# Half a crossed product on ScalarE and GpSimd, and an earlier issue of weights, in a convolution with a recurrent transformer behind it

## The chip, the cores and the metric

The kernel runs on one core of one Trainium2 chip. The metric is the device time of one execution in microseconds.

## The reference, cut to what matters

Two independent heads; their outputs are joined along the last axis. Head A is a transformer with a recurrent memory: 64 segments of 32 rows, one behind the other, each with 8 rows of memory that the segment before has left. Head B is a long convolution of `u` with a kernel that comes from a state-space model, done over the frequency domain, plus a skip.

```
# A: for s in range(64):
h = concat([mem, xs]);  q, k, v = h @ Wq, h @ Wk, h @ Wv      # 1024 -> 32 heads x 128
o = softmax(mask(q @ k.T * scale)) @ v;  o = o @ Wo           # 4096 -> 1024
mem = o[:, :8];  outs.append(o[:, 8:])
# B: L = 2048, D = 1024, N = 128
K = einsum(Cc, exp(dt * A * l), dt * Bc).real                 # [D, L]
y = irfft(rfft(pad(u.T)) * rfft(pad(K)))[:, :L].T + u * Dskip
```

## The kernel before, in words

The program is written out by hand: each engine does its instructions in the order in which the Python code issues them, and semaphores are added wherever an instruction reads or overwrites what an earlier one, in that order, has written or still reads. Head B comes first (`part_b`), with the projections of A's rows that need no memory woven in; head A follows (`part_a`, from about 577 us on).

In `part_b` the spectrum of `u` is made by matmuls and kept in DRAM (`Ud`); that of the convolution's kernel is made block by block: 16 blocks of 256 columns and a quarter of the frequencies (`b`, `dq`, `kc`). Each block has two pairs of frequency classes, `n_` = 0 and 1. The loop over `b` (L1542) does the following.

- `spectrum(b + 1, n_, ...)` (L1221) on TensorE: 20 matmuls into a PSUM tile `pa` of 128 x 1024 float32 (two banks, `ps_e` with two tiles and `ps_h` with one). The left operand is a forward matrix `G[kc]`, three fifths of which are scaled first on VectorE by `weighted` (L1206); that is done once for each `kc`, in blocks 0 to 3.
- `pointwise(b, now)` (L1461) is a generator in two stages. The first stage multiplies the block's spectra by that of `u`: `times_u` (L1384) makes for each pair the crossed product `Zs[:, n_]` (the imaginary part of `u` times the tile) and then, in place, the straight one. `rotate` (L1389) joins both into a complex product, for pair 0 into `even` (named `y` in the profile). `load_u` (L1214) then fetches `u` for the next block into `uq[0]` and `uq[1]` (`wq` in the profile). The second stage, behind a `yield`, rotates pair 1 in place, forms a difference (`od`) and a sum (`y`) on VectorE, and has GpSimd spread them into bfloat16 tiles `Bt` by four operations (L1486 to L1489).
- From block 4 on `inverses(b - 4, n_)` on TensorE goes back to time: 16 or more matmuls, the skip through an identity, and an eviction on ScalarE (L1538). ScalarE's queue also issues the store of the rows.
- `skips` on GpSimd multiplies rows of `u` by `Dskip`.

Where the second stage is run depends on the block. For `b < 3` it comes ahead of the second spectrum of `b + 1`; for `b >= 3` it comes behind both spectra.

SyncE's queue (SP) carries nearly all loads, in order: `u`'s spectrum, `u`'s rows for the skips (`load_pair`, L1496), the inverse matrices `MI`, and the weights of head A. These are 512 KB tiles that stay in SBUF for all segments; `residents` (L1679) is a generator that issues one at each `next(resident)`, into memory that head B has done with. Behind it come four streamed buffers `wst` (L1704 to L1706), then eight tiles in the place of `MI`.

In `part_a` a segment goes through `quads` for q, k and v and `oproj` for the output; `unit` (L300) gives the weight tile for a key, from SBUF or, for twelve keys, streamed from DRAM by `stage` (L337). In the first segment it also loads the resident tiles that had no room before. Three tiles are kept in PSUM as bits (`load_kept`, L343): for the key `("q", 0, 7)` the right half is kept so, through a `wst` buffer, and the left half lies in `a_half`. Both are loaded in the first segment, where the key `("q", 0, 2)` is asked for.

Of the kernel before, what the change touches and what calls it, by code (L numbers as in the profile page):

```python
# [10 lines left out]
BF16 = mybir.dt.bfloat16  # L11
F32 = mybir.dt.float32
I32 = mybir.dt.int32
I16 = mybir.dt.int16
ALU = mybir.AluOpType
# [249 lines left out]
def load_resident(tc, pool, src, key, W_res, eng=None, t_=None):  # L265
    if t_ is None:
        t_ = pool.tile([128, 2048], BF16, name="W_%s" % "_".join(str(i) for i in key))
    (eng or tc.nc.sync).dma_start(out=t_[:].rearrange("e (h d) -> e h d", h=2) if key[0] == "o" else t_[:], in_=src(key))
    W_res[key] = t_


def part_a(ctx, tc, x, src, WD, HE, seg_len, out_a, ahead, W_res, rest, places, first):
# [17 lines left out]
    ctx.enter_context(tc.manual_schedule())  # L290
    ctx_w = rest.ctx
    wst = ahead.wst
    wres = ctx_w.enter_context(tc.tile_pool(name="a_wres", bufs=1, side="right"))

    loads = [SLOTS]
# [4 lines left out]
    def unit(key):  # L300
        if key in rest:

            rest.remove(key)
            load_resident(tc, wres, src, key, W_res, None, places.pop(0)() if places else None)
        if key in W_res:
            return W_res[key]
        if key in KEPT:
            return ahead_of.pop(key) + halves.get(key, [])
        between.pop(key, lambda: None)()
        if key in first:  # L310
            return first.pop(key)
        if key[0] == "v":
            for k_ in rest[0:3 if key[1] == 0 else 1]:
                rest.remove(k_)
                load_resident(tc, wres, src, k_, W_res)
        return stage(key, WD[key][:])

    ctx_l = ctx_w.enter_context(ExitStack())
# [24 lines left out]
    def load_kept(key):  # L343
        kept[key] = {}
        for n in (1,) if key in HALF else (0, 1):
            kept[key][n] = ps_k.tile([128, 512], F32, name="keep", tag="keep%d" % sum(len(b) for b in kept.values()))
        if key in HALF:
            w = wst.tile([128, 2048], BF16, name="wst", tag="w%d" % (loads[0] % SLOTS))
            loads[0] += 1
            h_ = ahead.low["half"] if key[0] == "q" else wres.tile([128, 1024], BF16, name="Whalf")  # L350
            for n, t_ in ((1, w[:, 0:1024]), (0, h_[:])):
                nc.sync.dma_start(out=t_, in_=src(key)[:, n, :] if key[0] == "o" else src(key)[:, 1024 * n:1024 * n + 1024])
            words(kept[key][1][:], w[:, 0:1024])
            halves[key] = [(0, 1024, h_)]
        else:
            t_ = first.pop(key)
            for n in (0, 1):
                words(kept[key][n][:], t_[:, 1024 * n:1024 * n + 1024])
# [47 lines left out]
    for s in range(NS):  # L406
# [123 lines left out]
        a = quads("k", 0, (0, 2, 4, 6, 1, 3, 5, 7))  # L530
# [3 lines left out]
        a = quads("q", 0, range(0, 6))  # L534
# [178 lines left out]
def part_b(ctx, tc, u, A_re, A_im, B_re, B_im, C_re, C_im, log_dt, Dskip, out_b, ahead, copies, residents, first_state):  # L713
# [667 lines left out]
        t_ = pool.tile([128, 2, 512], F32, name="pa", tag="pa")  # L1381
        return [t_[:].rearrange("p h (c d) -> p h c d", c=2)]

    def times_u(s_, Z, n_, X=None):  # L1384
        us = uq[n_].rearrange("p (a c d) -> p a c d", a=2, c=2)
        for i, t_ in ((1, Z), (0, s_[n_][0] if X is None else X)):
            v.tensor_tensor(out=t_, in0=us[:, :, i, :].unsqueeze(2).to_broadcast([128, 2, 2, DQ]), in1=s_[n_][0], op=ALU.mult)  # L1387

    def rotate(Y, X, Z):  # L1389
        v.tensor_tensor(out=Y[:, :, 0, :], in0=X[:, :, 0, :], in1=Z[:, :, 1, :], op=ALU.subtract)  # L1390
# [45 lines left out]
    iv = ctx.enter_context(tc.tile_pool(name="b_iv", bufs=2))  # L1436
    bp = ctx.enter_context(tc.tile_pool(name="b_B", bufs=1))
    ctx2 = ctx.enter_context(ExitStack())
    pw = ctx2.enter_context(tc.tile_pool(name="b_pw", bufs=1))
    bp0 = ctx2.enter_context(tc.tile_pool(name="b_B0", bufs=1))  # L1440
    out_v = out_b.rearrange("(c p r) d -> r p c d", p=128, r=4)
    u_v = u.rearrange("(c p r) d -> r p c d", p=128, r=4)
# [3 lines left out]
    places = [wsl[3][:], wsl[0][:], g0[:, 6144:8192], XT[:, 2048:4096], XT[:, 0:2048]] + [g0[:, 2048 * i:2048 * i + 2048] for i in range(3)]  # L1446
    resident = residents(pool, places + [XT[:, 2048 * i:2048 * i + 2048] for i in range(2, 10)], [t_[:] for t_ in wsl[1:3]], [k1[:, 2048 * i:2048 * i + 2048] for i in range(2)])

    Zs, even = (pw.tile([128, *dims], F32, name=nm) for nm, dims in (("z", (2, 2, 2, DQ)), ("y", (2, 2, DQ))))

    def blocks(t_):
        return t_.rearrange("p i c d -> p (i c) d")
# [8 lines left out]
    def pointwise(b, s_):  # L1461
        dq, kc = b // 4, b % 4
        if b:
            times_u(s_, Zs[:, 0], 0)
            if b < 4:
                rotate(even, s_[0][0], Zs[:, 0])
                if b < 3:
                    weighted(b + 1, 0, amps[b + 1])
                load_u(b + 1, (0,))
                for i in {1: (0,), 2: (4,), 3: ()}[b]:  # L1470
                    load_inverse(i)
                if b == 1:
                    next(resident)
            times_u(s_, Zs[:, 1], 1)
            if b < 15:
                load_u(b + 1, (1,) if b < 4 else (0, 1))
            if b > 3:
                rotate(even, s_[0][0], Zs[:, 0])
        yield
        if b:  # L1480
            rotate(s_[1][0], s_[1][0], Zs[:, 1])
        Y = (even[:], s_[1][0]) if b else (first[:, 0], first[:, 1])
        v.tensor_tensor(out=odd[:], in0=Y[0], in1=Y[1], op=ALU.subtract)
        v.tensor_tensor(out=even[:], in0=Y[0], in1=Y[1], op=ALU.add)
        for i, op in ((0, ALU.add), (1, ALU.subtract)):
            gp.tensor_tensor(out=spectra(dq, kc, 0)[:, i], in0=even[:, 0], in1=even[:, 1], op=op)  # L1486
        eng, to = v if b == 15 else gp, blocks(spectra(dq, kc, 1))
        eng.tensor_tensor(out=to[:, 0:4:3], in0=odd[:, 0], in1=odd[:, 1, ::-1], op=ALU.add)
        eng.tensor_tensor(out=to[:, 2:0:-1], in0=odd[:, 0], in1=odd[:, 1, ::-1], op=ALU.subtract)  # L1489
# [52 lines left out]
    for b in range(16):  # L1542
        points = pointwise(b, now)
        next(points)
        for _ in range(4 if b in (2, 3) else 0):
            second.pop(0)()
        if b == 2:
            ks.append([])
        if 2 <= b < 6:
            lo, hi = b - 2, min(b - 1, 3) if b < 5 else 5  # L1550
            ks[1].extend(load_k(1, k1[:, DH * lo:DH * hi], lo))
        if b >= 4:
            load_pair(b - 2, iv)
        if b == 3:
            v.tensor_scalar(out=ident[:], in0=ident[:], scalar1=float(PLEN / 2), scalar2=None, op0=ALU.mult)
            load_pair(0, iv)
            load_pair(1, iv)
            state = first_state(g0[0:8, 5120:6144], iv.tile([128, 8, 24], BF16, name="xt0", bufs=1))
            next(state)
            ctx_k.close()  # L1560
            ps_h = ctx.enter_context(tc.tile_pool(name="b_psh", bufs=1, space=PSUM))
            ps_y = ctx.enter_context(tc.tile_pool(name="b_psy", bufs=2, space=PSUM))
        if b == 0:
            now = nxt_
        elif b + 1 < 16:
            now = []
            for n_ in range(2):
                if b < 3 and n_:
                    next(points, None)
                    weighted(b + 1, 1, amps[b + 1])  # L1570
                now.append(halves(ps_h if b > 2 and (2 * b + n_) % 3 == 0 else ps_e))
                spectrum(b + 1, n_, [now[n_][0][:, half] for half in range(2)], (3,) * 7 if b == 1 else ())
                if b >= 4:
                    inverses(b - 4, n_)
        next(points, None)
        for n_ in (0, 1) if b == 3 else (b - 2,) if 3 < b < 15 else ():
            skips(n_, gp)
        for i in {1: (1,), 3: (5,), 4: (2, 3), 5: (6, 7)}.get(b, ()):
            load_inverse(i)
        if b == 2:  # L1580
            rows4 = g0[0:4, 5120:6144]
            for half in range(2):
                sy.dma_start(out=rows4[:, DH * half:DH * half + DH], in_=Kx[half][31, NF - 1].rearrange("g c -> (g c)").partition_broadcast(4))
            sy.dma_start(out=w4, in_=u[0:4, :])
            gp.tensor_tensor(out=w4, in0=rows4[:, 0:D], in1=w4, op=ALU.mult)
            gp.memset(l4, 0.0)
            gp.memset(l4[:, :, 127:128], float(PLEN / 2))
            gp.affine_select(out=l4[:, :, 127:128], in_=l4[:, :, 127:128], compare_op=ALU.is_ge, fill=0.0, base=0, pattern=[[1, 4], [0, 1]],
                             channel_multiplier=-1)
        for _ in range({1: 2, 2: 2, 3: 1, 4: 1, 5: 1, 6: 2, 7: 2, 8: 2, 9: 2, 11: 3, 12: 3, 13: 2, 14: 3, 15: 3}.get(b, 0)):  # L1590
            next(resident)
        if b == 10:
            state.send(ps_y.tile([128, 8, 128], BF16, name="yp", tag="yp")[:, :, 0:8])
# [3 lines left out]
    for n_ in range(3):  # L1597
        inverse_begin(3, PAIRS[n_], begun[n_ // 2][:, n_ % 2])
    ctx2.close()
    last = ctx.enter_context(tc.tile_pool(name="b_last", bufs=1))  # L1600
    load_pair(14, iv)
    load_pair(15, last, 1)
    for _ in range(4):
        next(resident)
    for n_ in range(8):
        if n_ > 0 and n_ % 2 == 0:
            skips(12 + n_ // 2, v)
        inverses(12 + n_ // 2, n_ % 2)
        if n_ == 1:
            next(state)  # L1610
        next(resident)
# [32 lines left out]
def kernel(  # L1644
# [34 lines left out]
    def residents(stay, early, uqs, last):  # L1679
# [8 lines left out]
        for t_ in some(stay, "KT1", 2):  # L1688
            put(t_)
            yield  # L1690
        for t_ in early:
            put(t_)
            yield
        put(last[0])
# [79 lines left out]
```

## Time and profile before

| | |
|---|---|
| three runs | 1917.59, 1918.08, 1934.71 us; median 1918.08 |
| the profiled execution | 1915.11 us; span of its instructions 1913.4 us |
| busy, share of the span | PE 92%, DVE 71%, PEld 57%, ACT 48%, POOL 27% |
| mean granted TensorE clock | 0.986 |
| DMA | 594.21 MB, mean 311 GB/s |
| frequency loop, blocks 0 to 15 | about 405 to 560 us |
| head A's 64 segments | from about 577 us to the end |

In a row of the timeline stand the start in us from the span's start, the duration in us, the engine, the line of the kernel, the operation, what it writes and reads, shapes, how many instructions were merged, and in brackets how long the engine had been idle and what ended that. PE is TensorE, PEld its weight load, DVE VectorE, ACT ScalarE, POOL GpSimd, SP SyncE; a q behind the name is the engine's queue that issues a DMA. In a row of one line's instructions stand the shortest, median and longest duration in ns. In a row of the windows stand for each engine the busy us and the number of instructions, then the granted share of TensorE's clock, the share of the 16 DMA engines that were busy and what they moved in GB/s.

### The profile page before, as it was taken

The numbers are of one execution on the slowest core, as the hardware profiler recorded it, in microseconds if no ns is written. First come the engines' busy times: TensorE is split into PE (matmuls) and PEld (weight loads), VectorE is DVE, ScalarE is ACT, GpSimd is POOL, SyncE is SP. The second block draws the span as 40 slices with busy tenths as digits, with TensorE's granted clock in tenths as the row PEclk, the third lists the DMA queues.
The fourth block names the chain that finished last, engine by engine and source line by source line (L and its number), as shares of the span: only waits on it lengthen the run. The fifth ranks groups of instructions, "written<-read, shape, count | busy, mean of one in ns | idle before, by whom it ended". The sixth has DMA issues, their size and how long they took to land.

```text
span 1913.4 us, 73735 instructions
## 1 busy us (share of the span) xinstructions
PE 1768.3 (92%) x31563; PEld 1088.4 (57%) x31563; DVE 1349.7 (71%) x3367; ACT 921.2 (48%) x1655; POOL 514.4 (27%) x900
## 2 busy tenths in 40 slices
PE   8999999868986989999999999999999999999989
PEld 3666665546773555555555555555555555555554
DVE  8599999899973666666666666766666666666650
ACT  8799999860112434444343444444343444444420
POOL 2354544427770111111111111111111111212120
PEclk9999999898998999999999999999999999999999
DMA  7889898778799999999999999999999999999993
GB/s 220 238 236 266 258 276 249 219 220 293 258 306 357 348 322 342 341 345 337 344 353 344 338 350 351 336 355 343 340 348 354 330 345 346 346 340 347 352 335 95
DMA packets 341744, 594.21 MB, mean 311 GB/s; under 512 B 94100, under 2 KB 216476, under 8 KB 339368
## 3 DMA queue, kind: packets, MB, share of 16 engines
q1 hardware_dynamic: 297944, 534.99, 81.8%
q10 hardware_dynamic: 36816, 29.59, 4.8%
q0 software_dynamic: 6656, 24.92, 3.5%
q8 instruction: 247, 4.05, 0.8%
q14 instruction: 81, 0.66, 0.1%
HBM read 531.92 MB, written 71.63 MB: 315 GB/s over the span
## 4 chain that ended last, share of the span: by engine, by line
PE 46%; DMA 31%; DVE 12%; ACT 5%; issue 3%; POOL 2%; SPq 1%; DVEq 0%; POOLq 0%; ACTq 0%
PE acc L414 22%; DMA wst<-WD_v 11%; DMA wst<-WD_o 9%; PE pp L527 9%; DMA wst<-WD_q 3%; PE pe L667 3%; DMA wst<-WD_k 2%; PE tr L425 2%; PE pro L184 2%; DVE nr L1274 1%; PE pro L197 1%; DMA arena<-PKd 1%; PE pv L495 1%; DMA wq<-Ud 1%; DVE pa L1387 1%
## 5 line engine op out<-in xcount | busy, mean ns | idle before, releaser
L414 PEld LDWEIGHTS <-a_hT 128*32 128x32 bf16 x12351 | 329.6, 96 | 327.3 <-issue 76.1
L420 ACT CAST arena<-acc 128x512 bf16<-128x512 f32 x384 | 225.2, 586 | 395.1 <-PE acc L414 326.8
L414 PE MATMUL acc<-wst,a_hT 128*32 128x512 bf16 x2308 | 230.1, 382 | 35.3 <-DMA wst<-WD_v 26.1
L527 PEld LDWEIGHTS <-arena 128*32 128x32 bf16 x8256 | 215.4, 96 | 76.9 <-issue 53.6
L428 POOL COPY arena<-arena 128x128 bf16<-128x128 bf16 x128 | 37.6, 294 | 697.6 <-PE tr L425 364.9
L335 DVE TENSOR_SCALAR arena<-keep 128x256 int32<-128x256 int32 x508 | 174.3, 395 | 27.9 <-PE acc L414 27.9
L414 PE MATMUL acc<-XM,a_hT 128*32 128x512 bf16 x2560 | 184.2, 380 | 0.0
L414 PE MATMUL acc<-W,a_hT 128*32 128x512 bf16 x1536 | 132.8, 384 | 0.0
L197 PE MATMUL pro<-XM,wsl 128*128 128x512 bf16 x512 | 124.6, 387 | 2.6 <-DVE kst L206 1.5
L454 DVE TENSOR_REDUCE a_mx<-sc 128x4 f32<-128x160 f32 (+1 forms) x192 | 71.8, 374 | 74.2 <-PE sc L442 72.9
L527 PE MATMUL pp<-W_o,arena 128*32 128x256 bf16 x3584 | 121.7, 273 | 2.3 <-issue 2.2
L544 DVE COPY arena<-tr 128x512 bf16<-128x512 bf16 x64 | 27.2, 425 | 126.3 <-PE tr L425 126.3
L458 ACT ACTIVATE sc<-sc 128x160 f32<-128x160 f32 (+1 forms) x192 | 63.9, 333 | 106.5 <-DVE sc L455 106.0
L462 DVE TENSOR_REDUCE a_mx<-sc 128x4 f32<-128x160 f32 (+1 forms) x192 | 72.7, 379 | 55.2 <-ACT sc L458 54.9
L489 POOL TENSOR_TENSOR arena<-arena,a_BD 128x128 bf16<-128x128 bf16 x128 | 51.3, 401 | 211.5 <-DVE arena L472 201.3
L414 PE MATMUL acc<-W_q,a_hT 128*32 128x512 bf16 x1536 | 107.9, 379 | 0.0
L1274 DVE TENSOR_SCALAR nr<-ptt 128x456 f32<-128x456 int16 x128 | 80.3, 628 | 31.3 <-PE ptt L1252 28.3
L1266 ACT ACTIVATE E<-pa 128x648 bf16<-128x648 f32 x128 | 87.7, 712 | 16.9 <-PE pa L1258 15.2
L623 ACT CAST arena<-pp 128x128 bf16<-128x128 f32 x64 | 17.0, 266 | 154.8 <-DVE arena L623 154.8
L527 PE MATMUL pp<-wst,arena 128*32 128x256 bf16 x1536 | 76.4, 274 | 16.4 <-DMA wst<-WD_o 15.0
L513 ACT CAST arena<-pv 128x512 bf16<-128x512 f32 (+1 forms) x128 | 61.4, 479 | 59.6 <-PE pv L499 33.4
L425 PEld LDWEIGHTS <-arena 128*128 128x128 bf16 x1024 | 57.6, 98 | 54.8 <-issue 25.9
(334 smaller groups left out, 3967.7 us busy)
## 6 DMA issues: line engine op xcount, KB each, us to landing
wst<-WD_v SPq DMA_DIRECT2D x256, 512.0 KB
wst<-WD_k SPq DMA_DIRECT2D x192, 512.0 KB
wst<-WD_o SPq DMA_DIRECT2D x192, 512.0 KB
wst<-WD_q SPq DMA_DIRECT2D x128, 512.0 KB
Ud<-ux POOLq DMA_DIRECT2D x16, 1024.0 KB, 7.5
wq<-Ud SPq DMA_DIRECT2D x32, 512.0 KB
wsl<-in_A_Wk_dram SPq DMA_DIRECT2D x16, 512.0 KB
wsl<-in_A_Wv_dram SPq DMA_DIRECT2D x16, 512.0 KB
```

Of the source, the lines that this page charges most:

```text
L197: nc.tensor.matmul(a[:], lhsT=w[:, kc, 128 * j:128 * j + 128], rhs=xTl[:, kc, :, :].rearrange("p s k -> p (s k)"), start=(kc == 0), stop=( ...
L335: nc.vector.tensor_scalar(out=out.bitcast(I32), in0=in_.bitcast(I32), scalar1=0, scalar2=None, op0=ALU.bitwise_or)
L414: nc.tensor.matmul(a[32 * g:32 * g + 32, o_:o_ + rhs.shape[1]], lhsT=hT[:, kc, :], rhs=rhs, start=(kc == 0), stop=(kc == KC - 1), tile_pos ...
L420: nc.scalar.copy(out=q, in_=a[:])
L425: nc.tensor.transpose(out=p[:, hl, :, :].rearrange("p a b -> p (a b)"), in_=q[:, 128 * hl:128 * hl + 128], identity=ident[:])
L454: nc.vector.tensor_reduce(out=m_, in_=x, axis=AX.X, op=ALU.max)
L458: nc.scalar.activation(out=flat(sc, i), in_=flat(sc, i), func=ACT.Exp, scale=scale)
L462: nc.vector.tensor_reduce(out=m_, in_=x, axis=AX.X, op=ALU.add)
L513: copy(out=o[:, i:i + n], in_=p[:, i:i + n, :].rearrange("p a (g q) -> p a g q", g=4))
L527: nc.tensor.matmul(po[32 * qt:32 * qt + 32, o_:o_ + rhs.shape[1]], lhsT=oT[:, h % 4, (h % 16) // 4, :], rhs=rhs, start=False, stop=(h == 3 ...
L1266: sc.activation(out=T["E", r, e // 4][:, lo:lo + 8 * NE].rearrange("p (i c) -> p i c", i=2), in_=T.pop(("p", r, e))[:, :, 0:4 * NE], func= ...
L1274: v.tensor_scalar(out=T["n", r, e // 4][:, lo:lo + 8 * NT], in0=T.pop(("t", r, e))[:, 0:8 * NT].bitcast(I16)[:, 0:16 * NT:2], scalar1=floa ...
```

## The change

1. `times_u` makes for pair 1 only the first half of the crossed product on VectorE (`parts=1`). The other half, `Zs[:, 1, 1]`, is made by two new functions: `moved` has ScalarE copy that half of the spectrum from PSUM, and `shared` has GpSimd multiply it in place by `u`. For block 1 both are issued in the turn `b == 0`; for later blocks `moved` is issued behind the second spectrum of `b + 1`, and `shared` ahead of the second stage of block `b` from `b = 3` on, behind it for `b` = 1 and 2.
2. `weighted(b + 1, 0, ...)` in blocks 1 and 2 moves behind the products of both pairs; from block 4 on `load_u` of the first half is issued directly behind the products of pair 0.
3. `Zs` and `even` get pools of their own, `even` first. The four streamed buffers are issued ahead of the last two `load_pair`; the last of these uses the ring of four instead of a pool of its own.
4. The left half of `("q", 0, 7)` is loaded by `residents` in `part_b`, ahead of the sixth tile of `early`. The first five resident tiles that `part_a` loads beside streamed v tiles go to a new pool `a_wout`.

```diff
+    wout = ctx_w.enter_context(tc.tile_pool(name="a_wout", bufs=1, side="right"))
+    outs = [wout.tile([128, 2048], BF16, name="W_o", tag="W%d" % i) for i in range(5)]
...
-                load_resident(tc, wres, src, k_, W_res)
+                load_resident(tc, wres, src, k_, W_res, None, outs.pop(0) if outs else None)
...
-            for n, t_ in ((1, w[:, 0:1024]), (0, h_[:])):
+            for n, t_ in ((1, w[:, 0:1024]), (0, h_[:]))[0:1 if key[0] == "q" else 2]:
...
-    def times_u(s_, Z, n_, X=None):
+    def times_u(s_, Z, n_, X=None, parts=2):
         us = uq[n_].rearrange("p (a c d) -> p a c d", a=2, c=2)
-        for i, t_ in ((1, Z), (0, s_[n_][0] if X is None else X)):
-            v.tensor_tensor(out=t_, in0=us[:, :, i, :].unsqueeze(2).to_broadcast([128, 2, 2, DQ]), in1=s_[n_][0], op=ALU.mult)
+        for i, m, t_ in ((1, parts, Z), (0, 2, s_[n_][0] if X is None else X)):
+            v.tensor_tensor(out=t_[:, 0:m], in0=us[:, 0:m, i, :].unsqueeze(2).to_broadcast([128, m, 2, DQ]), in1=s_[n_][0][:, 0:m], op=ALU.mult)
+
+    def moved(s_):
+        sc.copy(out=Zs[:, 1, 1], in_=s_[1][0][:, 1])
+
+    def shared():
+        us = uq[1].rearrange("p (a c d) -> p a c d", a=2, c=2)
+        gp.tensor_tensor(out=Zs[:, 1, 1], in0=us[:, 1, 1, :].unsqueeze(1).to_broadcast([128, 2, DQ]), in1=Zs[:, 1, 1], op=ALU.mult)
...
-    pw = ctx2.enter_context(tc.tile_pool(name="b_pw", bufs=1))
+    py, pw = (ctx2.enter_context(tc.tile_pool(name="b_p%s" % nm, bufs=1)) for nm in "yw")
...
             times_u(s_, Zs[:, 0], 0)
+            if b > 3 and b < 15:
+                load_u(b + 1, (0,))
             if b < 4:
                 rotate(even, s_[0][0], Zs[:, 0])
-                if b < 3:
-                    weighted(b + 1, 0, amps[b + 1])
                 load_u(b + 1, (0,))
...
-            times_u(s_, Zs[:, 1], 1)
+            times_u(s_, Zs[:, 1], 1, parts=1)
             if b < 15:
-                load_u(b + 1, (1,) if b < 4 else (0, 1))
+                load_u(b + 1, (1,))
+            if b < 3:
+                weighted(b + 1, 0, amps[b + 1])
             if b > 3:
                 rotate(even, s_[0][0], Zs[:, 0])
...
         if b == 0:
             now = nxt_
+            moved(now)
+            shared()
         elif b + 1 < 16:
...
                 spectrum(b + 1, n_, [now[n_][0][:, half] for half in range(2)], (3,) * 7 if b == 1 else ())
+                if n_ and b + 1 >= 1:
+                    moved(now)
                 if b >= 4:
                     inverses(b - 4, n_)
+        if b > 2 and b < 15:
+            shared()
         next(points, None)
+        if 0 < b < 3 and b + 1 >= 1:
+            shared()
...
     ctx2.close()
-    last = ctx.enter_context(tc.tile_pool(name="b_last", bufs=1))
-    load_pair(14, iv)
-    load_pair(15, last, 1)
     for _ in range(4):
         next(resident)
+    load_pair(14, iv)
+    load_pair(15, iv)
...
-        for t_ in early:
+        for i, t_ in enumerate(early):
+            if i == 5:
+                tc.nc.sync.dma_start(out=ahead.low["half"][:], in_=src(("q", 0, 7))[:, 0:1024])
             put(t_)
             yield
```

More of the change, by code (lines that the diff above doesn't have):

```diff
@@ L1447, in part_b @@
     resident = residents(pool, places + [XT[:, 2048 * i:2048 * i + 2048] for i in range(2, 10)], [t_[:] for t_ in wsl[1:3]], [k1[:, 2048 * i:2048 * i + 2048] for i in range(2)])
-    Zs, even = (pw.tile([128, *dims], F32, name=nm) for nm, dims in (("z", (2, 2, 2, DQ)), ("y", (2, 2, DQ))))
+    even, Zs = (p.tile([128, *dims], F32, name=nm) for p, nm, dims in ((py, "y", (2, 2, DQ)), (pw, "z", (2, 2, 2, DQ))))
     def blocks(t_):
```

## The prediction

> **What bounds the kernel now.** I read the windows first. Between 440 and 560 us (blocks 4 to 15 of the frequency loop) VectorE works 98% of the time; behind it TensorE stands still.
>
> ```profile
> 480.00:500.00 20.00, 18.25 (x159) 15.13 (x157) 19.66 (x21) 2.39 (x4) 14.09 (x10) 1.00 0.82 270
> 560.00:600.00 40.00, 25.90 (x277) 15.46 (x276) 10.13 (x16) 10.20 (x17) 11.95 (x47) 0.83 0.95 327
> ```
>
> The columns are PE, PEld, DVE, ACT, POOL busy, then clock, DMA share, GB/s. Next the timeline of one steady block, for the order of work:
>
> ```profile
> 481.08 1.22 DVE L1484 TENSOR_TENSOR y<-y,pa 128x1024 f32<-128x1024 f32 x1
> 485.62 1.22 DVE L1387 TENSOR_TENSOR pa<-wq,pa 128x1024 f32<-128x1024 f32 x1
> 486.75 0.68 DVE L1390 TENSOR_TENSOR y<-pa,z 128x512 f32<-128x512 f32 x1
> 486.82 0.38 PE L1537 MATMUL yp<-uu,b_ident 128*128 128x512 bf16 x1
> 487.30 2.13 POOL L1503 TENSOR_TENSOR uu<-uu,Dsk 128x1024 bf16<-128x1024 bf16 x1
> 487.29 0.60 ACT L1538 ACTIVATE uu<-yp 128x512 bf16<-128x512 f32 x1 [3.60 <-PE yp L1537]
> 487.35 0.68 DVE L1391 TENSOR_TENSOR y<-pa,z 128x512 f32<-128x512 f32 x1
> 487.94 0.69 DVE L1390 TENSOR_TENSOR pa<-pa,z 128x512 f32<-128x512 f32 x1
> 488.08 2.34 PE L1227 MATMUL pa<-k,XM 128*128 128x256 bf16 x20 [0.88 <-DVE y L1391]
> 490.73 1.22 DVE L1484 TENSOR_TENSOR y<-y,pa 128x1024 f32<-128x1024 f32 x1
> 491.87 1.21 DVE L1387 TENSOR_TENSOR z<-wq,pa 128x1024 f32<-128x1024 f32 x1
> 492.09 2.50 POOL L1486 TENSOR_TENSOR Bt<-y 128x512 bf16<-128x512 f32 x2 [2.66 <-DVE y L1484]
> ```
>
> A block is four products (L1387), two rotations of two instructions each (L1390, L1391), a difference and a sum. The sum starts at 481.08 and again at 490.73: a block lasts 9.65 us. The second rotation (487.94) follows the first without a gap, before the second spectrum of the next block (488.08) has even begun.
>
> At the seam to the recurrent part the bound is DMA. TensorE's waits there (total us, times, longest):
>
> ```profile
> PE acc L414 <- DMA a_half<-in_A_Wq_dram: 11.1, 1, 11.1
> PE acc L414 <- DMA wst<-WD_v: 6.6, 2, 5.6
> 617.25 0.23 PE tro L629
> 636.45 0.23 PE tro L629
> ```
>
> The two lower rows, of the chain that ended last, are the ends of the first two of the 64 segments: 19.2 us apart. The change edits nothing in a later segment.
>
> **The change part by part.** (1) *The saved half product.* z of pair 1 shrinks from 1024 to 512 elements. Durations:
>
> ```profile
> L1387 DVE TENSOR_TENSOR z<-wq,pa x30: 1206/1215/1221, 405.5 to 552.0; 128x1024 f32<-128x1024 f32 x30
> L1390 DVE TENSOR_TENSOR y<-pa,z x15: 684/684/693, 408.6 to 554.3; 128x512 f32<-128x512 f32 x15
> L1042 ACT COPY ua<-ups x32: 566/586/589, 68.7 to 363.5; 128x512 f32<-128x512 f32 x32
> L1016 POOL TENSOR_TENSOR ux<-us x16: 1263/1266/1269, 83.6 to 372.3; 128x512 f32<-128x512 f32 x16
> ```
>
> A 128x512 product of PSUM and SBUF takes 0.68 where the whole takes 1.21, so VectorE saves 0.53 us a block. For it ScalarE copies 512 columns (as L1042, 0.59) and GpSimd multiplies them in place (as L1016, 1.27).
>
> (2) *The wait that this adds.* There is one Zs for all blocks. From block 3 on the program order is: products and first rotation of block b, both spectra of b+1, the copy into Zs[:,1,1] for b+1, GpSimd's product there, and only then (the second next(points)) the second rotation of b, which reads all of Zs[:,1]. A read that comes behind a write in program order waits for it. So the rotation that now starts at 487.94 is held by a chain through three engines: the second spectrum of b+1 (starts 0.05 behind the first rotation, whose end is 487.35 + 0.68 = 488.03, and takes 2.34), ScalarE (0.09 later, from 486.82 + 0.38 to 487.29, then 0.59), GpSimd (0.08, as from 490.73 + 1.22 + 0.14 to 492.09, then 1.27), and 0.08 back. It starts 0.05 + 2.34 + 0.09 + 0.59 + 0.08 + 1.27 + 0.08 = 4.50 behind that end, 4.59 later than now. Queued behind it on VectorE are the difference, the sum and all of the next block; behind the sum wait GpSimd's four Bt operations and the next spectrum on TensorE. Net 4.59 - 0.53 = 4.06 a block. Nothing covers it: the products of b+1 stand behind it in the queue. GpSimd is free in time: four Bt operations (two take 2.50) and the skip (2.13) end some 7.2 us into the block; the chain needs it at 8.4 (products 3 x 1.13 + 0.60, rotation 1.28, then 0.05 + 2.34 + 0.09 + 0.59 + 0.08). Blocks 4 to 14: 11 x 4.06 = **44.7**. Bounds of the 4.59: 4.3 without the semaphore steps, 5.5 if the multiply waits for u's load.
>
> (3) *The start.* For block 1 the copy and the multiply are issued ahead of block 0's Bt operations on GpSimd:
>
> ```profile
> 406.03 2.50 POOL L1486 TENSOR_TENSOR Bt<-y 128x512 bf16<-128x512 f32 x2 [26.86 <-PE pa L1227]
> 406.66 2.72 ACT L1178 ACTIVATE XM<-gf 128x512 bf16<-128x512 int16 x5
> 408.56 0.69 DVE L1390 TENSOR_TENSOR y<-pa,z 128x512 f32<-128x512 f32 x1 [0.74 <-POOL Bt L1486]
> L1209 DVE TENSOR_TENSOR XM<-XM,wq x6: 949/952/2037, 398.1 to 430.9; 128x1536 bf16<-128x1536 bf16 x6
> 438.68 0.69 DVE L1390 TENSOR_TENSOR pa<-pa,z 128x512 f32<-128x512 f32 x1
> ```
>
> ScalarE has five sines ahead of the copy (to 409.4), so the copy ends at 410.0, the multiply at 411.3, Bt at 413.8. The first rotation of block 1 overwrites y, which Bt reads; it waited 0.74 already and now starts at 413.9, not 408.6. The weighting that moves behind both products no longer runs beside GpSimd: 0.95 for 2.04 in blocks 1 and 2. Of the 5.3 some 3.7 are left behind block 1 and 2.5 behind block 2. Block 3's rotation (438.68) is held as in (2), about 4.2 net with its own small operations on GpSimd: 2.5 + 4.2 = **+6.7** at the first product of block 4, bounds 2 and 8.
>
> (4) *The clock.* The block grows to 13.7 us while TensorE's work stays 18.25 / 20 x 9.65 = 8.8, so it idles 4.9, of which some 3.9 in one piece, from behind the second spectrum and its inverse to the next block. Windows of 3.41 us:
>
> ```profile
> 440.84:444.26 3.42, 1.75 (x17) 1.38 (x15) 3.39 (x4) 0.00 (x0) 1.50 (x2) 1.00 0.43 131
> 447.67:451.09 3.42, 1.24 (x11) 1.01 (x11) 3.26 (x5) 0.60 (x1) 3.42 (x3) 1.00 0.98 347
> 451.09:454.50 3.41, 3.41 (x19) 2.35 (x17) 2.44 (x3) 0.00 (x0) 2.90 (x3) 0.50 1.08 321
> 560.32:563.73 3.41, 1.75 (x11) 0.98 (x11) 3.10 (x3) 0.60 (x1) 3.41 (x8) 1.00 0.33 95
> 563.73:567.14 3.41, 3.41 (x16) 2.28 (x15) 1.38 (x2) 1.20 (x2) 2.81 (x12) 0.50 0.88 235
> 450.07 3.49 PE L1227 MATMUL pa<-XM 128*128 128x256 bf16 x20
> ```
>
> Windows with 1.24 and 1.75 us of work (447.67, 560.32) are each followed by one at 0.50; that at 440.84, with 1.75, was not. So the limit lies near half a window. The twenty matmuls straddling that drop took 3.49, not 2.34. An idle stretch of 3.9 puts at least 1.95 into one window, which leaves at most 1.46 of work there, so a slow window follows in nearly every block. It costs up to 3.41 x 0.5 = 1.7 us of TensorE time; some 0.4 is slack ahead of the second spectrum (0.88 in the steady block, less 0.53), the rest delays the chain: 1.2 a block, 11 x 1.2 = **13**; bounds 0 (it falls wholly into idle time) and 20. The Trainium skill, "TensorE: Matmul & The Clock Gate", in Part 1: The HAM clock gate, has the half rate set in only after a whole idle window of about 3.4 us. By that rule a 3.9 us gap would hold a whole free-running window only about once in seven blocks and the 13 would be about 2; this trace drops the clock after windows that had work in them, so I go by the trace.
>
> (5) *Block 15* has no next product, so it keeps its saving (0.5), and the one wait for u (below, 1.0 us) is covered: **-1.5**.
>
> ```profile
> 453.28 1.22 DVE L1387 TENSOR_TENSOR z<-wq,pa 128x1024 f32<-128x1024 f32 x1 [0.95 <-DMA wq<-Ud]
> ```
>
> Issuing u's first half apart from its second costs nothing: SP issued it 2.3 us before the other already.
>
> (6) *The seam.*
>
> ```profile
> 561.02 2.25 SPq L1498 DMA_DIRECT2D uu<-in_B_u_dram  x2
> 563.32 0.50 SPq L1706 DMA_DIRECT2D wst<-in_A_Wk_dram  x1
> 561.00:566.00 5.00, 4.02 (x21) 2.43 (x21) 3.44 (x4) 1.79 (x3) 4.54 (x15) 0.77 0.59 159
> 576.93 0.40 PE L414 MATMUL acc<-Wlow,a_hT 128*32 128x512 bf16 x4
> 590.79 0.69 DVE L335 TENSOR_SCALAR keep<-wst 128x512 int32<-128x512 int32 x1 [11.83 <-DMA wst<-in_A_Wq_dram]
> 591.43 0.61 PE L414 MATMUL acc<-a_half,a_hT 128*32 128x512 bf16 x2 [11.07 <-DMA a_half<-in_A_Wq_dram]
> ```
>
> SP stood in front of u's last loads until 561 while DMA ran at 159 GB/s; four buffers of 512 KB queued behind. Issued first they fill the hole, (327 - 159) GB/s x 5 us = 0.84 MB, 2.6 us at the 327 of the stretch. The early half (256 KB) frees another 0.8. It does not remove the 11 us stall alone: the other half of the same weights landed at 590.8 too. What is late next is that half. But the slower blocks give DMA slack: loads are issued by block, each now 15 us instead of 9.65, so the backlog at the seam (estimated at up to 3 MB, 9 us) is gone. The last buffers still wait for TensorE's inverses, which end at 576.93. I take **-9**, bounds -3 and -13. u's last two loads move behind the four buffers and the last into the ring of four; the inverses that use them are the last ones ahead of 576.93, so I cost that at nothing, 2 us if they come later. The five W_o tiles move to a pool of their own: same bytes, nothing.
>
> *Sum*, against the profiled execution's own 1915.1 (span 1913.4): 44.7 + 6.7 + 13 - 1.5 - 9 = +54, 1969. The runs shown have their median 3 us higher, at 1918.1: I put **1970**.
>
> **Rivals.** *A: held, but at full clock* (idle stretches cut by inverses that start late): 1970 - 13 = 1957. For it: 440.84 with 1.75 of work kept 1.00. Against: the gap here is wider.
>
> *B: u's load is late as well.* The multiply of b+1 needs u's second half, issued when the last product ends, some 4.4 us before it is wanted; a landing a microsecond or two late adds 1.5 x 11: 1986. The 1.0 us wait at 453.28 speaks for it, the lighter DMA load per block against.
>
> *C, the other side: not held.* If the rotation of b runs ahead of the copy for b+1, VectorE's 0.53 stands as a gain in 15 blocks (TensorE's 8.8 does not bind): 8, the weightings 2, the seam 3.4, the start +3.7: 1915 - 10, with the 3 us of the runs 1908. It decides where the rotation's start is nearer to 0 than 0.5 us behind the first rotation. The program order above speaks against it. This is also the case in which the change does what its words say.
>
> **How the numbers follow.** Forecast 0.62; A 0.18; B 0.10; C 0.07; 0.03 for a mix. The forecast's bounds: low 2 + 42 + 0 - 1.5 - 13 = +30, 1945; high 8 + 47 + 20 - 1.5 - 3 = +70, 1985, both from the profiled time; with A and most of B inside, 1945 to 1988 leaves out C and little else. Slower by over 1% (19 us, about what a measurement of this kernel tells from no change): forecast, A, B and most of the mix, 0.92. The 0.08 that are left are C and its neighbours; the whole VectorE gain plus the whole 11 us stall make just 19 us, so 0.02 is faster by over 1% and 0.06 within it.
>
> **What would show it.** In the profile after: L1390's second rotation with some 4 us or more of idle time before each, released by GpSimd's multiply, in twelve blocks; z of pair 1 at 0.68; the block at 14 to 16 us; windows at clock 0.5 in the loop; the first rotation of block 1 waiting about 5 us for Bt; the wait for a_half gone and a shorter one for the other half in its place. Wrong if the second rotation still follows the first at once, or the segments behind the seam change their 19 us.

## The result and the profile after

The changed kernel is slower: 1983.06 us, median of six runs (1978.97 to 1985.69), against 1917.84 for the kernel before on the same chip (six runs, 1916.84 to 1934.71). The ratio is 1.0309, its 95% interval 1.0287 to 1.0331. The forecast was 1970 in a range of 1945 to 1988. The profiled execution of the changed kernel took 1985.69 us, 70.6 more than that of before, with a span of 1984.0 and a mean granted clock of 0.965.

The windows of the changed kernel, in the columns of the first fence of the prediction:

```profile
480.00:500.00 20.00, 12.92 (x84) 9.75 (x84) 13.59 (x15) 1.78 (x3) 10.06 (x8) 0.77 0.53 173
```

In the same 20 us VectorE now works 13.59 where it worked 19.66, and every other engine works less as well. No engine has become the bound: all of them wait. The timeline of one steady block says for what:

```profile
481.40 1.22 DVE L1495 TENSOR_TENSOR y<-y,pa 128x1024 f32<-128x1024 f32 x1
482.68 4.43 PE L1229 MATMUL pa<-XM 128*128 128x256 bf16 x20 [4.96 <-DVE y L1495]
484.81 0.68 DVE L1389 TENSOR_TENSOR z<-wq,pa 128x512 f32<-128x512 f32 x1
484.92 2.21 SPq L1218 DMA_DIRECT2D wq<-Ud  x2
487.26 0.68 DVE L1400 TENSOR_TENSOR y<-pa,z 128x512 f32<-128x512 f32 x1
489.12 2.35 PE L1229 MATMUL pa<-XM 128*128 128x256 bf16 x20
491.54 0.59 ACT L1392 COPY z<-pa 128x512 f32<-128x512 f32 x1 [1.63 <-PE pa L1229]
492.85 1.26 POOL L1396 TENSOR_TENSOR z<-wq,z 128x512 f32<-128x512 f32 x1 [3.12 <-DMA wq<-Ud]
494.14 0.70 DVE L1399 TENSOR_TENSOR pa<-pa,z 128x512 f32<-128x512 f32 x1 [6.21 <-POOL z L1396]
496.87 1.22 DVE L1495 TENSOR_TENSOR y<-y,pa 128x1024 f32<-128x1024 f32 x1
```

L1495 is the sum that was L1484 before, L1389 the product, L1399 and L1400 the rotation. The first rotation ends at 487.94. The second can start only at 494.14, behind the second spectrum of the next block (489.12), ScalarE's copy (491.54) and GpSimd's multiply (492.85). VectorE stands 6.21 us, and the sum comes again 15.47 us behind the last one.

VectorE's waits in the changed kernel (us in total, times, longest):

```profile
DVE pa L1399 <- POOL z L1396: 68.9, 12, 6.6
```

The twelve waits are those of blocks 3 to 14.

Three pairs of rows place the whole difference. First the sum of blocks 1 to 15, before and after (the first and the last start stand behind the durations), then that of blocks 3 to 14 alone, then the last step of the first 63 segments:

```profile
L1484 DVE TENSOR_TENSOR y<-y,pa x15: 1220/1220/1221, 416.9 to 558.2; 128x1024 f32<-128x1024 f32 x15
L1495 DVE TENSOR_TENSOR y<-y,pa x15: 1220/1220/1223, 421.6 to 625.7; 128x1024 f32<-128x1024 f32 x15
L1484 DVE TENSOR_TENSOR y<-y,pa x12: 1220/1220/1221, 441.5 to 548.6; 128x1024 f32<-128x1024 f32 x12
L1495 DVE TENSOR_TENSOR y<-y,pa x12: 1220/1220/1223, 450.7 to 616.5; 128x1024 f32<-128x1024 f32 x12
L629 PEld LDWEIGHTS <-arena x126: 95/95/105, 617.0 to 1831.0; 128*128 128x128 bf16 x126
L631 PEld LDWEIGHTS <-arena x126: 95/96/96, 680.6 to 1900.8; 128*128 128x128 bf16 x126
```

| stretch | before | after | difference | forecast |
|---|---|---|---|---|
| to the sum of block 1 | 416.9 | 421.6 | +4.7 | +3.7 |
| blocks 2 and 3 | 24.6 | 29.1 | +4.5 | +3.0 |
| blocks 4 to 14 | 107.1 | 165.8 | +58.7 | +56.7 |
| block 15 | 9.6 | 9.2 | -0.4 | -0.5 |
| last sum to the end of segment 1 | 58.8 | 54.9 | -3.9 | -9 |
| 62 further segments | 1214.0 | 1220.2 | +6.2 | 0 |

A block of the loop takes 165.8 / 11 = 15.07 us where it took 107.1 / 11 = 9.74. The 56.7 is made of 44.7, 13 and the 1.0 of waiting for `u` that was to go. The last line belongs to code that the change does not touch. In the profiles of the seven kernels below, the same 62 segments took 1202.1 to 1224.4, so the 6.2 lies within the scatter of single executions.

At the seam, TensorE's waits and the issues of SP:

```profile
PE acc L416 <- DVE arena L337: 7.5, 1, 7.5
624.48 0.33 SPq L1726 DMA_DIRECT2D wst<-in_A_Wk_dram  x1
626.34 2.25 SPq L1509 DMA_DIRECT2D uu<-in_B_u_dram  x2
```

The 11.1 us wait for `a_half` is gone, and one of 7.5 for the other half of the same weights (L337 unpacks it) stands in its place. The buffers are now issued ahead of `u`'s last loads.

### The profile page after: what moved, and what is told of

Read it like the earlier page. It is cut to its first block, busy times and chain, and to the rows that moved or that the text cites. A ratio compares the mean times of both kernels' runs of the same rounds, so it can differ in the third digit from the quotient of the medians.

```text
span 1984.0 us, 73783 instructions
## 1 busy us (share of the span) xinstructions
PE 1789.5 (90%) x31563; PEld 1097.5 (55%) x31563; DVE 1341.4 (68%) x3367; ACT 928.2 (47%) x1670; POOL 529.8 (27%) x915
## 4 chain that ended last, share of the span: by engine, by line
PE 45%; DMA 30%; DVE 14%; ACT 5%; issue 3%; POOL 2%; ACTq 0%; SPq 0%; POOLq 0%; DVEq 0%
PE acc L416 22%; DMA wst<-WD_v 11%; DMA wst<-WD_o 11%; PE pp L529 7%; PE pe L669 3%; DMA wq<-Ud 2%; DMA wst<-WD_q 2%; PE tr L427 2%; DMA arena<-PKd 2%; DMA wst<-WD_k 2%; DVE nr L1276 2%; PE pa L1229 1%; PE pro L184 1%; PE pro L197 1%; PE ptt L1254 1%
## 5 line engine op out<-in xcount | busy, mean ns | idle before, releaser
L337 DVE TENSOR_SCALAR arena<-keep 128x256 int32<-128x256 int32 x508 | 174.1, 394 | 29.6 <-PE acc L416 29.5
L1276 DVE TENSOR_SCALAR nr<-ptt 128x456 f32<-128x456 int16 x128 | 80.3, 627 | 32.1 <-PE ptt L1254 29.1
L1229 PEld LDWEIGHTS <-XM 128*128 128x128 bf16 x480 | 55.0, 116 | 78.2 <-issue 41.6
```

Of the source, the lines that this page charges most:

```text
L337: nc.vector.tensor_scalar(out=out.bitcast(I32), in0=in_.bitcast(I32), scalar1=0, scalar2=None, op0=ALU.bitwise_or)
L1229: pe.matmul(outs[half][:, cs, :], lhsT=G[kc][:, n_, j, cs, half, :], rhs=KT[j][:, d], start=(j == 0), stop=(j == 4), skip_group_check=True)
L1276: v.tensor_scalar(out=T["n", r, e // 4][:, lo:lo + 8 * NT], in0=T.pop(("t", r, e))[:, 0:8 * NT].bitcast(I16)[:, 0:16 * NT:2], scalar1=floa ...
```

## The experiments

The theory: the block grew because the second rotation of `b` is issued behind a write of `Zs[:, 1, 1]` for `b + 1`, and nothing else. Its rival: the chain over three engines is too slow in itself, or the other edits cost the time. The first four kernels separate these; the last three separate what lengthens the chain.

### The second rotation issued ahead of the copy

```diff
...
             rotate(s_[1][0], s_[1][0], Zs[:, 1])
+        if 2 < b < 15:
+            yield
...
-                if n_ and b + 1 >= 1:
+                if n_:
+                    if b > 2:
+                        next(points)
                     moved(now)
```

> The whole change, but the second rotation of block b is issued ahead of the copy for block b+1 (from block 3 on); nothing else is moved, no buffer is added. Theory 1 (the loss is the wait that the program order adds on the one Zs): the second rotation follows the first at once, a block falls from 15.1 us to 9.1 to 9.9 us, the time to 1905 to 1925; the 3.5 us at block 1 stay. Theory 2 (the new work itself slows the block: ScalarE's extra reads of PSUM, GpSimd's extra 1.3 us a block): a block stays above 12 us and the time above 1950.

Measured: 1920.69 us, ratio to before 1.0005 (0.9981 to 1.0030). The same instructions, with two of them in another place of the order, bring back 62 us (1983.06 - 1920.69); by the starts of the sum, 57.3 of them lie in blocks 4 to 14 (165.8 - 108.5) and 5.0 in block 3. The rows of this kernel (sum, two instructions of the timeline, waits of GpSimd and VectorE between 440 and 560):

```profile
L1497 DVE TENSOR_TENSOR y<-y,pa x12: 1220/1220/1223, 446.6 to 555.1; 128x1024 f32<-128x1024 f32 x12
494.64 0.68 DVE L1400 TENSOR_TENSOR y<-pa,z 128x512 f32<-128x512 f32 x1
495.24 0.69 DVE L1399 TENSOR_TENSOR pa<-pa,z 128x512 f32<-128x512 f32 x1
POOL z L1396 <- DMA wq<-Ud: 15.3, 10, 3.2
DVE y L1399 <- POOL Bt L1499: 3.8, 4, 1.4
DVE z L1389 <- DMA wq<-Ud: 2.5, 2, 2.1
```

The second rotation (495.24) again follows the first at once. A block takes 108.5 / 11 = 9.86 on average, not less than the 9.74 of before, though VectorE has less to do in it. Seven of the eleven blocks take 9.24, where a steady block took 9.65; the other four take 9.84 to 12.88. Most of their extra is in two waits. GpSimd's multiply stands in front of the Bt operations in its queue and is itself held up by `u` (GpSimd stands 15.3 us in ten blocks), so Bt comes late, and the next first rotation, which overwrites what Bt reads, waits for it (3.8). VectorE's own products wait 2.5 for `u`, where they waited 1.0 before.

### The multiply also placed between GpSimd's other operations

On top of the edit above, the multiply for block 1 goes behind block 0's Bt operations, and from block 3 on between the Bt pair that reads the sum and the pair that reads the difference. For that, `pointwise` stops once more between the two pairs. The lines are shown against the changed kernel.

```diff
...
             gp.tensor_tensor(out=spectra(dq, kc, 0)[:, i], in0=even[:, 0], in1=even[:, 1], op=op)
+        if 2 < b < 15:
+            yield
...
         if b == 0:
             now = nxt_
             moved(now)
-            shared()
...
-        if b > 2 and b < 15:
-            shared()
         next(points, None)
-        if 0 < b < 3 and b + 1 >= 1:
+        if 2 < b < 15:
+            shared()
+            next(points, None)
+        if b < 3:
             shared()
```

> As the run with the order alone, and two more moves: block 1's multiply is issued behind block 0's operations on GpSimd, and from block 3 on the multiply stands between the two Bt operations that read the sum and the two that read the difference. Theory 1: a block near 9.1 us (VectorE's own work), the first rotation of block 1 waits under 1 us instead of 5.8, time 1900 to 1910, some 3 to 12 us below the run with the order alone. Rival (u's second half lands about 6 us behind its issue and holds the multiply, and so GpSimd, whatever the order): a block stays at 9.6 or above and the time at 1912 or above.

Measured: 1910.24 us, ratio to before 0.9941 (0.9914 to 0.9969). This version beats both kernels, the one before by 0.6%, with an interval clear of 1.

```profile
L1497 DVE TENSOR_TENSOR y<-y,pa x15: 1220/1220/1221, 415.4 to 553.0; 128x1024 f32<-128x1024 f32 x15
L1497 DVE TENSOR_TENSOR y<-y,pa x12: 1220/1220/1221, 439.6 to 543.8; 128x1024 f32<-128x1024 f32 x12
408.35 0.69 DVE L1399 TENSOR_TENSOR y<-pa,z 128x512 f32<-128x512 f32 x1 [0.74 <-POOL Bt L1499]
POOL z L1396 <- DMA wq<-Ud: 0.4, 1, 0.4
DVE z L1389 <- DMA wq<-Ud: 2.5, 1, 2.5
```

By the time GpSimd comes to the multiply, `u` has landed (0.4 us of waiting in place of 15.3), and a block takes 104.2 / 11 = 9.47 on average. The starts of the single sums divide this: ten blocks take 9.24, which is 0.41 less than the 9.65 of before, and one takes 11.79, since its first product waits 2.5 for `u`; the same block took 10.69 before, with a wait of 1.0. So `u` no longer holds GpSimd, but still VectorE once. The average lies between what the two theories had said (near 9.1, or 9.6 and above), and the time just above the 1910 of the first. The first rotation of block 1 waits 0.74 as it did before, and block 1's sum starts at 415.4 where it started at 421.6; 1.5 of these 6.2 lie ahead of block 1, in the start of block 0's sum (404.1 for 405.6).

### The other edits alone

Part 1 of the change is undone: the whole crossed product is VectorE's again, nothing is copied or multiplied elsewhere.

```diff
...
-            times_u(s_, Zs[:, 1], 1, parts=1)
+            times_u(s_, Zs[:, 1], 1)
...
```

> The change without its first part: the crossed product is whole on VectorE again, nothing is copied or multiplied elsewhere; the moved weighting, the split issue of u, the pools, the four buffers ahead of u's last loads, the early half and the new pool for W_o stay. If the loss lies in the crossed product alone: 1911 to 1918 (seam -3, weighting -2). If the moved loads or the new places of the tiles cost too: 1925 or more.

Measured: 1916.67 us, ratio to before 0.9979 (0.9952 to 1.0006): no difference that can be told.

```profile
L1494 DVE TENSOR_TENSOR y<-y,pa x15: 1220/1220/1221, 417.9 to 559.2; 128x1024 f32<-128x1024 f32 x15
L1494 DVE TENSOR_TENSOR y<-y,pa x12: 1220/1220/1221, 442.6 to 549.5; 128x1024 f32<-128x1024 f32 x12
L631 PEld LDWEIGHTS <-arena x126: 95/96/96, 614.1 to 1832.9; 128*128 128x128 bf16 x126
```

Blocks 4 to 14 take 106.9, against 107.1 before. The seam, from the last sum to the end of segment 1, takes 614.1 - 559.2 = 54.9, the same as in the changed kernel, though the blocks here are fast.

### The product and the weighting alone

The opposite: the edits of the pools, of the order behind the loop and of the early half are undone, parts 1 and 2 stay. The lines show the order behind the loop.

```diff
...
+    last = ctx.enter_context(tc.tile_pool(name="b_last", bufs=1))
+    load_pair(14, iv)
+    load_pair(15, last, 1)
     for _ in range(4):
         next(resident)
-    load_pair(14, iv)
-    load_pair(15, iv)
...
```

> The first two parts of the change alone (crossed product, weighting, u's issue); pools, four buffers, early half and W_o as before. The seam in the changed kernel is about 4 us shorter than before. If that comes from the loads having more time in the slower blocks: the seam is shorter here too, 1978 to 1985. If it comes from the earlier issue: the seam is as before and the time 1984 to 1990.

Measured: 1987.63 us, ratio to before 1.0348 (1.0306 to 1.0390). Its rows: the sum, segments, SP's issues, five microseconds behind the loop, and TensorE's longest wait at the seam.

```profile
L1493 DVE TENSOR_TENSOR y<-y,pa x12: 1220/1220/1220, 450.8 to 615.6; 128x1024 f32<-128x1024 f32 x12
L629 PEld LDWEIGHTS <-arena x126: 95/96/98, 683.9 to 1908.3; 128*128 128x128 bf16 x126
621.47 8.41 SPq L1507 DMA_DIRECT2D uu<-in_B_u_dram  x2
629.93 0.50 SPq L1723 DMA_DIRECT2D wst<-in_A_Wk_dram  x1
626.10:631.10 5.00, 2.08 (x9) 1.06 (x10) 4.52 (x4) 0.60 (x1) 4.85 (x9) 0.62 0.12 36
PE acc L414 <- DMA a_half<-in_A_Wq_dram: 10.9, 1, 10.9
```

The blocks are as slow as in the changed kernel (164.8 / 11 = 14.98). The sum of block 15 starts at 624.9 here, so the seam takes 683.9 - 624.9 = 59.0, as before (58.8). The seam gets nothing of the slow blocks. Behind the last of them SP stands until 629.9 in front of `u`'s last loads, 5.1 us behind the last sum, as before (563.3 - 558.2); while it stands, the DMA moves only 36 GB/s. The 10.9 us wait for `a_half` remains.

### TensorE filled, u's other half read, and both

What makes the wait 5.7 us long on average (68.9 / 12), where 4.50 was forecast? Two answers fit the timeline above: the second spectrum starts late since the first one ran at half clock (4.43 us), or the multiply waits for `u`. The first kernel puts 24 unused matmuls behind the inverses of blocks 4 to 14, so that the clock stays up; the second lets the multiply read the half of `u` that is issued earlier, so that its product is not the one that the reference asks for; the third does both.

```diff
+        if 3 < b < 15:
+            fill = ps_y.tile([128, 2, DQ], F32, name="yp", tag="yp")
+            for i in range(24):
+                pe.matmul(fill[:, i % 2, :], lhsT=MI[0][:, 0, 0, 0, :], rhs=...)
         if b > 2 and b < 15:
             shared()
```

```diff
     def shared():
-        us = uq[1].rearrange("p (a c d) -> p a c d", a=2, c=2)
+        us = uq[0].rearrange("p (a c d) -> p a c d", a=2, c=2)
```

> The changed kernel with 24 more matmuls of 256 columns (into a PSUM tile that nothing reads) behind each block's inverses, blocks 4 to 14, so that TensorE is busy while VectorE is held. In the changed kernel the second spectrum starts 0.89 us behind the first rotation on average, not 0.05, and GpSimd's multiply starts 0.62 behind the copy, not 0.08. Theory K (the slow clock alone delays the chain): the clock stays at 1.00, the spectrum starts at once, the block falls by 0.8 to 14.2 us and the time by 9 us against the changed kernel. Theory U (u's second half, landing some 6 us behind its issue, holds the multiply in most blocks whatever the clock does): the clock is mended but the block falls by 0.4 us or less and the time by under 5 us.

> The changed kernel, but GpSimd multiplies by the half of u that was loaded first (pair 0's; so the crossed product of that half isn't the one wanted). It takes the wait for the second load away and leaves the clock as it is. Theory U: the multiply starts 0.08 behind the copy, the block falls by 0.5 to 14.5 us, the time by 6 us against the changed kernel. Theory K: no change, 15.1 us.

> Both together. If clock and load are all that lengthens the chain beyond its own operations, the hold falls from 5.8 us to 4.5, the block to 13.7 or 13.8 us and the time by 15 us against the changed kernel, to about 1968; if a block stays above 14.2 us, something else is in it (the filling matmuls themselves, or GpSimd).

Measured: 1979.86, 1978.65 and 1975.12 us; ratios to before 1.0301 (1.0262 to 1.0340), 1.0298 (1.0264 to 1.0331) and 1.0276 (1.0231 to 1.0321). The intervals overlap, so the whole times alone decide nothing; the loop is read from the rows. For the changed kernel and these three, in that order, the windows of 149 us, and for the three the sum of blocks 3 to 14:

```profile
451.00:600.00 149.00, 107.63 (x758) 82.40 (x759) 88.80 (x98) 17.90 (x31) 85.32 (x62) 0.83 0.60 193
```

```profile
451.00:600.00 149.00, 119.79 (x987) 98.56 (x998) 90.32 (x99) 18.00 (x31) 85.44 (x62) 0.95 0.60 196
L1495 DVE TENSOR_TENSOR y<-y,pa x12: 1220/1220/1223, 452.1 to 617.0; 128x1024 f32<-128x1024 f32 x12
```

```profile
451.00:600.00 149.00, 108.67 (x775) 84.83 (x786) 95.31 (x105) 17.90 (x31) 89.50 (x66) 0.85 0.59 194
L1495 DVE TENSOR_TENSOR y<-y,pa x12: 1220/1220/1221, 449.6 to 608.3; 128x1024 f32<-128x1024 f32 x12
```

```profile
451.00:600.00 149.00, 122.44 (x1031) 101.61 (x1042) 100.33 (x110) 18.60 (x32) 91.39 (x68) 0.97 0.63 205
L1495 DVE TENSOR_TENSOR y<-y,pa x12: 1220/1220/1223, 453.8 to 606.5; 128x1024 f32<-128x1024 f32 x12
```

The last two columns are averages over blocks 4 to 14 from the timelines: how long behind the first rotation's end the second spectrum starts, and how long behind the end of ScalarE's copy GpSimd's multiply starts.

| kernel | clock | a block | saved a block | spectrum late | multiply late |
|---|---|---|---|---|---|
| changed | 0.83 | 165.8 / 11 = 15.07 | | 0.89 | 0.62 |
| filled | 0.95 | 164.9 / 11 = 14.99 | 0.08 | 0.31 | 1.13 |
| other half of `u` | 0.85 | 158.7 / 11 = 14.43 | 0.64 | 0.78 | 0.08 |
| both | 0.97 | 152.7 / 11 = 13.88 | 1.19 | 0.24 | 0.08 |

The clock alone gives nearly nothing: the spectrum starts 0.58 earlier, and the multiply waits 0.51 longer for `u` behind the copy. `u` alone gives half, since the late spectrum then decides. Only both give the 1.19. They are two waits side by side, and the later one counts. The filling itself holds nothing: behind the 24 matmuls TensorE still stands 2.1 to 3.3 us before the next spectrum in the blocks from 480 to 515. With both gone, ten of the eleven blocks take 13.70 each; block 4, whose spectrum is late in all four kernels, takes 15.7. The whole time of the last kernel, 1975.12, misses the 1968 that was expected, though its eleven blocks gave 13.1 us; the rest of the program scatters (its 62 segments took 1223.9 in the profiled execution, 3.7 more than in the changed kernel).

## Why the prediction was right, and where not

**Step 1, the saved half product: real, but 0.41 and not 0.53.** z of pair 1 takes 0.68 (484.81), as worked out. What counts in a queue is the step from one start to the next, and there the two rows behind differ (before and after):

```profile
484.48 1.22 DVE L1387 TENSOR_TENSOR z<-wq,pa 128x1024 f32<-128x1024 f32 x1
485.52 1.23 DVE L1389 TENSOR_TENSOR pa<-wq,pa 128x1024 f32<-128x1024 f32 x1
```

The whole product is followed 1.14 behind its start by the next one (485.62), the half one 0.71 behind its start (485.52); the prediction had put 1.13 and 0.60. That is the 0.41 by which a block without waits is shorter with the better order (9.24 for 9.65).

**Step 2, the hold: right in mechanism and size.** Program order with one `Zs` makes the second rotation of `b` wait for the multiply of `b + 1`, in twelve blocks. Removing that order removes the loss (1920.69). With clock and `u` out of the way the second rotation starts 4.44 behind the first one's end, where 4.50 was worked out, and ten of the eleven blocks take 13.70, where 9.65 + 4.06 gives 13.71. That it fits so closely is partly luck: the saving was put 0.12 too large, the hold 0.06 too long, and the step from the second rotation to the difference fell from 0.80 to 0.73 besides.

**Step 3, the start: right in kind, 2.5 us short** (+9.2 at block 4 for +6.7).

The start of the changed kernel in the timeline:

```profile
411.19 1.26 POOL L1396 TENSOR_TENSOR z<-wq,z 128x512 f32<-128x512 f32 x1 [31.25 <-ACT z L1392]
412.41 2.47 POOL L1497 TENSOR_TENSOR Bt<-y 128x512 bf16<-128x512 f32 x2
414.92 0.69 DVE L1399 TENSOR_TENSOR y<-pa,z 128x512 f32<-128x512 f32 x1 [5.85 <-POOL Bt L1497]
417.97 0.95 DVE L1211 TENSOR_TENSOR XM<-XM,wq 128x1536 bf16<-128x1536 bf16 x1
```

The multiply goes ahead of Bt, the rotation waits 5.85 for it, and the weighting takes 0.95, all as written. The rotation starts 1.0 later than the 413.9 of the working, but not by the change: block 0's sum, ahead of all this, already starts at 405.58 for 404.33, and in the nine profiles it starts anywhere from 404.1 to 407.1. From that sum to the next, the change costs 3.5 (16.05 for 12.56) where 3.7 was worked out, and block 3 costs 4.1 (15.86 for 11.74) where it was 4.2. The term that failed is block 2. It was to save 1.2 and takes 13.20 for 12.83, 0.4 more. VectorE has two waits there that it had not before:

```profile
DVE z L1389 <- ACT z L1392: 1.3, 1, 1.3
DVE z L1389 <- PE pa L1229: 0.6, 1, 0.6
```

The moved weighting does take 0.95 for 2.04, but it ends later, TensorE stands 2.14 until 418.98 for it in the middle of block 2's first spectrum and then runs slower (0.85 for three matmuls that took 0.49 before), and block 2's first product waits for that spectrum: 0.6 here, 1.2 in the kernel with the other edits alone. The other 1.3 is a wait of pair 1's product for ScalarE's copy. The prediction put both at nothing.

**Step 4, the clock: the sum was right, the cause only half.** The clock falls in every block as forecast. Windows of the changed kernel, in the steps of 3.41 us in which its clock changes:

```profile
477.17:480.58 3.41, 0.55 (x4) 0.25 (x4) 1.83 (x3) 0.60 (x1) 1.26 (x1) 1.00 1.05 393
480.58:484.00 3.42, 1.32 (x7) 0.95 (x7) 3.39 (x4) 0.00 (x0) 1.30 (x2) 0.50 0.51 174
484.00:487.41 3.41, 3.41 (x18) 2.43 (x17) 3.38 (x5) 0.00 (x0) 3.41 (x3) 0.50 0.42 114
487.41:490.82 3.41, 3.41 (x32) 2.95 (x31) 0.53 (x1) 0.60 (x1) 2.32 (x2) 1.00 0.77 202
```

A window with 0.55 us of work is followed by one at 0.50, and that one, with 1.32 of work, by a second at 0.50. By the rule of the Trainium skill that the prediction weighed ("TensorE: Matmul & The Clock Gate", Part 1), the half rate sets in after a whole idle window. This trace differs: the window from 477.17 was not wholly idle, and the measurement decides. I put the 1.2 us a block down to this alone. The filled kernel shows that it is worth 0.08 by itself: rival B, `u`'s late landing, given 0.10, was true at the same time and covered it. In the block shown, `u`'s second half is issued in the stretch that starts at 484.92, and the multiply still waits for it until 492.85, 0.72 us behind the end of the copy. The forecast took the two as alternatives of which one adds to the other; they lie in parallel. Together they are the 1.19 that one of them was to cost, so that the 13 us came out near right by luck. The measured 1983 is nearer to rival B's 1986 than to 1970, but not for B's reason: the 16.5 that B adds did not appear, blocks 4 to 14 came within 2.0 of the forecast.

**Step 5: right.** Block 15 keeps 0.4 of the forecast 0.5.

**Step 6, the seam: -3.9 for -9.** The failed part is the slack that the slower blocks were to give the DMA. The edits alone were worked out at 3.4 (2.6 for the hole, 0.8 for the early half), and the kernel with blocks of 9.72 (106.9 / 11) gains just 3.9 by them. The other 5.6 came from a guess that a backlog of loads would be worked off in the slow loop; no row showed that backlog. The kernel with slow blocks and without these edits gains nothing (59.0 for 58.8), and with the edits the seam takes 53.4 and 57.4 in the two versions with the better order and 54.3 to 57.3 in the last three kernels, whose blocks are slow: the loads ahead of the seam are not late for want of DMA, they are issued late, since SP stands in front of `u`'s last loads. The wait that was named as late next, for the other half of the same weights, is there with 7.5 us.

The errors of steps 3 and 6 are 2.5 and 5.1, that of blocks 4 to 14 is 2.0, the 62 segments brought 6.2, and 0.9 lies in block 15 and the last segment: so the profiled execution came to 1985.7 where the sum had given 1969.

## What to carry to other kernels

Where one scratch buffer serves all turns of a loop, work handed to other engines for the next turn must be issued behind the last read of this turn: two instructions moved in the order were worth 62 us here, and the place of the multiply in GpSimd's queue another 10. Two waits that end near one another are not added and not chosen between: take one away and the other is left, so an experiment has to take away each and both. A transfer that is late because its issue is late gains nothing from an idle DMA.

## What the runs showed of the hardware

The unchanged part of 62 segments took between 1202.1 and 1224.4 us in nine profiled executions of kernels that agree in it, 1.8%, which is more than most of the effects studied. Single kernels scatter as much: 27 runs of the kernel before took 1909.70 to 1931.40. The cause of this is open, and differences below 1% had to be read from the loop's own rows. In the profiled execution of the best version these segments took 1202.1, so its 1896 us in that execution are not its 1910.24 of the median.
